# A spectral mix with a gated feed-forward block on one core: fewer first-layer passes for the value banks, and a fixed order of instructions

## The chip, the core and the metric

The kernel runs on one core of a Trainium2 chip. The metric is the device time of one execution in microseconds. TensorE multiplies matrices and accumulates in PSUM, which has eight banks here; VectorE, ScalarE and GpSimd work on elements (GpSimd on SBUF only); SyncE (SP) issues most of the DMA transfers. Each engine works through its own queue in order. An instruction that waits for another engine or for a transfer holds all that stands behind it in its queue.

## The reference

For each of 8 batches, x has 3008 rows of 256 columns:

```python
X = fft(fft(x, axis=1), axis=2);  y = X.real             # (8, 3008, 256)
g, v = y @ w_gate, y @ w_val                             # 256 -> 1536
out = (0.5*g*(1 + erf(g/sqrt(2))) * v) @ w_out           # 1536 -> 256
```

For real x the result has a symmetry: the spectrum at a row k and at the mirrored row 3008 - k share their parts. If E is the part of a gate or a value that is even in the columns and O the odd part, then row k has E + O, and the mirrored row has E - O, apart from one column of the odd half, the Nyquist column N (it lies in partition 0), which keeps its sign. So half of the rows, 1505 of them, suffice to compute both.

## The kernel before, in words

**Transform.** The rows of x are folded with their columns' mirror images (`fold_x`), on GpSimd in the main loop. The transform along the rows is done in two steps on TensorE: `a_step` (12 of them for a batch; lines 308 to 323) multiplies slices of the folded x (`xf`) with a table `G`, and the result goes by way of PSUM bank `ps_d` into `S1`. `z_write` writes `S1` to DRAM in eight transfers, four after the sixth step and four after the twelfth, and `z_read` reads it back, turned, into `Ap` in two transfers (the first holds the groups 0 to 15, the second 16 to 31). `b_steps` (lines 346 to 395) multiplies `Ap` with small tables and copies the result into `Y`, which has an even half and an odd half of 1505 columns.

**Feed-forward block.** The transform along the columns is multiplied into the weights at the start (`gen_w`): `WE` for the even half, `WOP` for the odd half, and `WOM`, which is -2 times `WOP` in all partitions but partition 0, where it is zero. The columns of `Y` are taken in three chunks of 512, 512 and 481. A *unit* is one batch, one chunk and one of 12 slices of the 1536 hidden columns; there are 8 x 3 x 12 = 288 units, 36 to a batch. `p1` computes the gate and the value for the plus rows, each as one pass with `WE` and one with `WOP` (lines 415 and 417), then GELU on ScalarE and the product on VectorE (lines 420 and 421) into `h`. `p2`, one unit later, adds one pass with `WOM` to each of the same two banks (line 431), which turns E + O into E - O, and again GELU and product (lines 435 and 436). So a unit has six first-layer passes on TensorE and two operations each on ScalarE and VectorE.

**Second layer.** When a chunk's 12 units are done, 96 matmuls of 256 columns (line 462) multiply `h` with the output weights; eight of them are put behind each of the next 12 units. After each 24, the result is copied by ScalarE and stored in four or five transfers.

**The next batch beside it.** While batch b is in the feed-forward block, units 0 to 11 each issue an `a_step` of batch b + 1, units 12 and 13 its `z_read`, and units 18 to 33 its `b_steps`, which are put between the unit's passes (`fill`). x of batch b + 2 is loaded and folded at units 0, 12 and 24, in pieces of eight slices.

**Order.** The order in which the program is written is not the order of the queues: a planner sorts the instructions of each engine by priority and by the time at which it expects them to be ready. So before the change a transform step whose data are late is planned behind other units' passes. Buffers: two PSUM banks for gates, three for values, two for the second layer, one for `ps_d`; two `h`, four `gl` (the GELU results), three `xin`.

Of the kernel before, what the change touches and what calls it, by code (L numbers as in the profile page):

```python
# [28 lines left out]
def kernel(  # L29
# [49 lines left out]
    Wo_sb = const_pool.tile([128, NFC, C], BF16)  # L79
    xf_bufs = [const_pool.tile([128, HJ, 2, 128], BF16, name=f"xf{i}") for i in range(2)]  # L80
# [31 lines left out]
    def gl_tile():  # L112
        return work.tile([128, 512], BF16, tag="gl", bufs=4, name="gl")
# [19 lines left out]

    xins = {}
# [17 lines left out]
    def fold_x(b, i, eng):  # L152
        j0, nj = PIECES[i]
        xt = xins[(b, i)]
        xf = xf_bufs[b % 2]
        parts = [(0, 128, 0, nj)]
        if j0 + nj == HJ:
            parts = [(0, 128, 0, nj - 1), (0, N1, nj - 1, 1)]
        for (p0, pn, s0, sn) in parts:
            o0 = (j0 + s0) * C  # L160
            lo = _sub(xt, [[C, sn], [1, 127]], s0 * C + 1, p0, pn)
            hi = _sub(xt, [[C, sn], [-1, 127]], s0 * C + 255, p0, pn)
            ea = _sub(xf, [[C, sn], [1, 127]], o0 + 1, p0, pn)
            od = _sub(xf, [[C, sn], [1, 127]], o0 + 129, p0, pn)
            eng.tensor_tensor(ea, lo, hi, op=ALU.add)  # L165
            eng.tensor_tensor(od, lo, hi, op=ALU.subtract)  # L166
            eng.tensor_copy(
                _sub(xf, [[C, sn], [128, 2]], o0, p0, pn),
                _sub(xt, [[C, sn], [128, 2]], s0 * C, p0, pn),
            )  # L170
# [35 lines left out]
    def scratch(n, name):  # L206
        return work.tile([128, n], FP32, tag=name, bufs=1, name=name)
# [75 lines left out]
    def gen_w():  # L283
        nc.vector.tensor_scalar(col_m, col_p, 1.0, -2.0, op0=ALU.is_ge, op1=ALU.mult)
        for i in range(2):
            wb = work.tile([128, NCH, F], BF16, tag="gw", bufs=2, name="wb")
            for t in range(NCH):
                wst["last"] = nc.gpsimd.tensor_copy(wb[:, t, :], wst[i][:, t, :])
            for f0 in range(0, F, 512):
                for eo in range(2):  # L290
                    ps = (ps_g, ps_v)[eo]()
                    for t in range(NCH):
                        nc.tensor.matmul(
                            ps, CW[:, t, eo, :], wb[:, t, f0 : f0 + 512],
                            start=(t == 0), stop=(t == NCH - 1))
                    if eo == 0:
                        nc.scalar.activation(WE[:, i, f0 : f0 + 512], ps, AF.Copy)
                    else:
                        nc.scalar.activation(WOP[:, i, f0 : f0 + 512], ps, AF.Copy)
                        nc.vector.tensor_scalar(  # L300
                            WOM[:, i, f0 : f0 + 512], WOP[:, i, f0 : f0 + 512], col_m, None,
                            op0=ALU.mult)

# [4 lines left out]
    def a_step(b, k):  # L308
# [6 lines left out]
        for i in range(2):  # L315
            jj = 2 * k + i
            st[b]["mm"] = nc.tensor.matmul(  # L317
                ps[:, i * C : (i + 1) * C], G[:, jj, :], _sub(xf, [[1, C]], jj * C),
                start=True, stop=True)
        dst = _sub(S1, [[1, 2 * C]], 2 * k * C)  # L320
        if k % 2:
            return nc.scalar.activation(dst, ps, AF.Copy)  # L322
# [23 lines left out]
    def b_steps(b, eo, q):  # L346
# [3 lines left out]
        def mm(gi, m1):  # L350
            def run():
# [9 lines left out]
                if g == 0:  # L361
                    t = T0P if even else T0Q
                    nc.tensor.matmul(ps[r, 0:N2], w, t[:, 0:N2], start=True, stop=True)
                    nc.tensor.matmul(ps[r, 8 * N2 : 8 * N2 + 1], w, t[:, N2 : N2 + 1],
                                     start=True, stop=True)
                else:
                    s = (36 * g) % N2
                    t = TP if even else TQ
                    nc.tensor.matmul(ps[r, o : o + N2], w, t[:, s : s + N2], start=True, stop=True)  # L369
            return run  # L370

        def evac():
# [5 lines left out]
            nc.vector.tensor_copy(  # L378
# [4 lines left out]
            nc.vector.tensor_copy(  # L383
                _sub(Y, [[32, n2], [1, 8 - f]], eo * YW + 32 * MID + g0 + f - 1),
                _sub(ps, [[1, n2], [N2, 8 - f]], MID + f * N2))
            if q == 0:
                nc.vector.tensor_copy(
                    _sub(Y, [[32, n2]], eo * YW + 32 * MID + 31), ps[:, MID:N2])
                nc.vector.tensor_copy(
# [15 lines left out]
    def p1(u, fill):  # L405
        b, ci, fc = units[u]
        c0, n = CH[ci]
        if fc == 0:
            hs[(b, ci)] = h_tile()
        h, Y = hs[(b, ci)], Ys[b]  # L410
        pg, pv = ps_g(), ps_v()
        banks[u] = (pg, pv)
        fs = slice(fc * 128, (fc + 1) * 128)
        for i, ps in enumerate((pg, pv)):
            nc.tensor.matmul(ps[:, :n], WE[:, i, fs], Y[:, 0, c0 : c0 + n], start=True, stop=False)  # L415
            fill()
            nc.tensor.matmul(ps[:, :n], WOP[:, i, fs], Y[:, 1, c0 : c0 + n], start=False, stop=True)  # L417
            fill()
        gl = gl_tile()
        nc.scalar.activation(gl[:, :n], pg[:, :n], AF.Gelu)  # L420
        nc.vector.tensor_tensor(h[:, fc, :n], gl[:, :n], pv[:, :n], op=ALU.mult)  # L421

    def p2(u, fill):
        b, ci, fc = units[u]
        c0, n = CH[ci]
        n -= n % 32
        h, Y = hs[(b, ci)], Ys[b]
        pg, pv = banks.pop(u)
        fs = slice(fc * 128, (fc + 1) * 128)
        for i, ps in enumerate((pg, pv)):  # L430
            nc.tensor.matmul(ps[:, :n], WOM[:, i, fs], Y[:, 1, c0 : c0 + n],  # L431
                             start=False, stop=True, skip_group_check=True)
            fill()
        gl = gl_tile()
        nc.scalar.activation(gl[:, :n], pg[:, :n], AF.Gelu)  # L435
        nc.vector.tensor_tensor(  # L436
            _sub(h, [[-1, n]], fc * 1024 + 512 + n - 1), gl[:, :n], pv[:, :n], op=ALU.mult)
# [6 lines left out]
    def l2_steps(b, ci):  # L444
# [5 lines left out]
        for sign in range(2):  # L450
            for pair in range(2):
                box = {}
                for s in range(2):
                    sub = 2 * pair + s
                    M = min(128, (n if sign == 0 else 32 * nm) - sub * 128)
                    for fc in range(NFC):
                        def run(sign=sign, pair=pair, s=s, sub=sub, M=M, fc=fc, box=box):
                            if "ps" not in box:
# [3 lines left out]
                            nc.tensor.matmul(  # L462
                                ps[:M, s * C : (s + 1) * C],
                                h[:, fc, sign * 512 + sub * 128 : sign * 512 + sub * 128 + M],
                                Wo_sb[:, fc, :], start=(fc == 0), stop=(fc == NFC - 1))
# [4 lines left out]
        def finish(sign, pair, M, ps):  # L470
            t = osb_tile()
            if M == 128:
                nc.scalar.activation(_sub(t, [[1, 2 * C]], 0), ps, AF.Copy)  # L473
            else:
                nc.scalar.activation(t[:, 0, :], ps[:, :C], AF.Copy)
                nc.scalar.activation(t[:M, 1, :], ps[:M, C:], AF.Copy)
# [46 lines left out]
    for q in range(4):  # L523
        for eo in range(2):
# [3 lines left out]
            evac()  # L528

# [3 lines left out]
    for u in range(NU + 1):  # L533
# [3 lines left out]
        if u < NU:  # L537
            if i % 12 == 0 and i < 36 and b + 2 < B:
                load_x(b + 2, i // 12)
                fold_x(b + 2, i // 12, nc.gpsimd)  # L540
            if b + 1 < B:
                if i < 12:
                    a_step(b + 1, i)
                    if i % 6 == 5:
                        z_write(b + 1, 2 * (i - 5), 12)
                elif i in (12, 13):
                    z_read(b + 1, 16 * (i - 12), 16)
                elif 18 <= i < 34:
                    k = i - 18
# [21 lines left out]

        if u < NU:
            p1(u, fill)
        if u > 0:
            p2(u - 1, fill)
# [4 lines left out]
        if u > 0 and u % 12 == 0:  # L580
            pb, pi = divmod(u // 12 - 1, 3)
            l2q += l2_steps(pb, pi)
        for _ in range(8 if u < NU else len(l2q)):
            if l2q:
                l2q.pop(0)()
# [30 lines left out]
```

## Time and profile before

| | |
|---|---|
| median of 3 runs | 739.55 us (735.27 to 741.46) |
| span of the profiled execution | 732.0 us (no other time is given for it) |
| TensorE busy | 695.4 us, 95% |
| VectorE, ScalarE, GpSimd busy | 473.2, 424.1, 113.1 us |
| chain of work that ended last | TensorE 92%, DMA 3%, VectorE 2% |
| passes of the first layer | 6 x 288, busy 108 us a line and bank |
| second layer, line 462 | 2304 matmuls, 298.6 us |

PE is TensorE, PEld its weight loads, DVE VectorE, ACT ScalarE, POOL GpSimd, SP SyncE. A row of a group gives line, engine, operation, output <- inputs, shapes and count, then the total busy time in us, the mean of one in ns, and the idle time in front of it with what ended it. Matmuls are pipelined: the duration of one (0.38 us) is longer than the distance to the next, so the distance of the starts gives the throughput. A row of the table by stage gives the stretch, its length, the busy time and count of each engine, then the TensorE clock granted (1.00 is full), the busy share of the DMA engines and GB/s. A row of the timeline gives start, duration, engine, line and operation. For SP the duration is that of issuing, not of the transfer.

### The profile page before, as it was taken

How to read it: one execution, taken by the hardware profiler on the slowest of the kernel's cores; microseconds unless marked ns; L12 is line 12 of the kernel's file. 1: busy time of each engine (PE TensorE's matmuls, PEld its weight loads, DVE VectorE, ACT ScalarE, POOL GpSimd, SP SyncE). 2: the span in 40 equal slices, each digit the busy share in tenths (PEclk: the TensorE clock that was granted, in tenths of full speed). 3: DMA queues.
4: the chain of work that ended last, by engine and by line, in shares of the span. 5: the costliest groups of instructions: out<-in, count | busy, mean ns of one | idle time of the engine just before them, and what ended most of it. 6: DMA issues, size and time to landing. Idle time of an engine off the chain costs nothing.

```text
span 732.0 us, 13929 instructions
## 1 busy us (share of the span) xinstructions
PE 695.4 (95%) x5040; PEld 439.7 (60%) x5040; DVE 473.2 (65%) x854; ACT 424.1 (58%) x761; POOL 113.1 (15%) x105
## 2 busy tenths in 40 slices
PE   1389999999999999999999999999999999999997
PEld 0145566666666666666666666666566666666666
DVE  7848676666667566666766666666666667665651
ACT  2347655666556655665556655566556665556662
POOL 1328220202205004400252003400000000000000
PEclk9989999999999999999999999999999999999999
DMA  8995841554444624544455535236111441111112
GB/s 180 275 240 131 216 98 30 143 136 123 98 114 117 169 64 121 123 116 126 100 141 137 142 88 130 56 85 167 35 39 35 123 121 43 30 44 41 43 45 69
DMA packets 63620, 79.29 MB, mean 108 GB/s; under 512 B 8256, under 2 KB 58432, under 8 KB 59456
## 3 DMA queue, kind: packets, MB, share of 16 engines
q1 hardware_dynamic: 61456, 74.48, 40.9%
q10 hardware_dynamic: 544, 3.15, 1.2%
q0 software_dynamic: 1552, 0.79, 0.9%
q8 instruction: 39, 0.64, 0.4%
q14 instruction: 29, 0.24, 0.1%
HBM read 41.94 MB, written 37.22 MB: 108 GB/s over the span
## 4 chain that ended last, share of the span: by engine, by line
PE 92%; DMA 3%; DVE 2%; SPq 1%; issue 0%; ACT 0%; ACTq 0%; DVEq 0%
PE ps_o L462 34%; PE ps_g L417 9%; PE ps_v L415 9%; PE ps_v L417 9%; PE ps_g L431 9%; PE ps_g L415 9%; PE ps_v L431 8%; PE ps_d L369 4%; PE ps_d L317 3%; DMA Ap<-z 2%; DMA xin<-in_x_dram 1%; SPq L334 1%; DMA z<-S 1%; DVE xf L166 0%; DVE xf L165 0%
## 5 line engine op out<-in xcount | busy, mean ns | idle before, releaser
L421 DVE TENSOR_TENSOR h<-gl,ps_v 128x512 bf16<-128x512 bf16 (+1 forms) x288 | 195.2, 678 | 214.4 <-ACT gl L420 102.5
L462 PE MATMUL ps_o<-Wo_sb,h 128*128 128x256 bf16 (+2 forms) x2304 | 298.6, 272 | 0.0
L462 PEld LDWEIGHTS <-h 128*128 128x128 bf16 (+2 forms) x2304 | 227.1, 100 | 81.8 <-issue 0.2
L420 ACT ACTIVATE gl<-ps_g 128x512 bf16<-128x512 f32 (+1 forms) x288 | 169.6, 589 | 169.3 <-PE ps_g L417 153.7
L436 DVE TENSOR_TENSOR h<-gl,ps_v 128x512 bf16<-128x512 bf16 (+1 forms) x288 | 194.1, 674 | 6.7 <-ACT gl L435 1.5
L435 ACT ACTIVATE gl<-ps_g 128x512 bf16<-128x512 f32 (+1 forms) x288 | 169.6, 589 | 35.6 <-PE ps_g L431 28.6
L415 PE MATMUL ps_g<-Y,WE 128*128 128x512 bf16 (+1 forms) x288 | 108.4, 377 | 0.7 <-ACT gl L435 0.3
L417 PE MATMUL ps_g<-Y,WOP 128*128 128x512 bf16 (+1 forms) x288 | 108.6, 377 | 0.0
L415 PE MATMUL ps_v<-Y,WE 128*128 128x512 bf16 (+1 forms) x288 | 108.4, 376 | 0.0
L417 PE MATMUL ps_v<-Y,WOP 128*128 128x512 bf16 (+1 forms) x288 | 108.3, 376 | 0.0
L431 PE MATMUL ps_g<-Y,WOM 128*128 128x512 bf16 (+1 forms) x288 | 107.8, 375 | 0.0
L431 PE MATMUL ps_v<-Y,WOM 128*128 128x512 bf16 (+1 forms) x288 | 107.5, 373 | 0.0
L165 POOL TENSOR_TENSOR xf<-xin 128x1016 bf16<-128x1016 f32 (+2 forms) x28 | 50.4, 1801 | 329.1 <-DMA xin<-in_x_dram 161.0
L431 PEld LDWEIGHTS <-WOM 128*128 128x128 bf16 x576 | 51.0, 97 | 51.4
L417 PEld LDWEIGHTS <-WOP 128*128 128x128 bf16 x576 | 56.1, 97 | 33.4 <-issue 3.6
L415 PEld LDWEIGHTS <-WE 128*128 128x128 bf16 x576 | 56.2, 98 | 30.9 <-issue 0.7
L473 ACT ACTIVATE osb<-ps_o 128x512 f32<-128x512 f32 x80 | 47.8, 597 | 42.6 <-PE ps_o L462 39.6
L369 PEld LDWEIGHTS <-Ap 96*128 96x128 bf16 (+1 forms) x744 | 39.8, 92 | 43.6 <-issue 24.4
L166 POOL TENSOR_TENSOR xf<-xin 128x1016 bf16<-128x1016 f32 (+2 forms) x28 | 50.4, 1800 | 0.0
L369 PE MATMUL ps_d<-TP,Ap 96*128 96x47 bf16 (+1 forms) x465 | 39.3, 185 | 1.8 <-DMA Ap<-z 1.7
L322 ACT ACTIVATE S<-ps_d 128x512 bf16<-128x512 f32 x42 | 25.0, 596 | 18.9 <-PE ps_d L317 18.9
L317 PEld LDWEIGHTS <-G 128*128 128x128 bf16 x192 | 19.5, 103 | 26.4 <-ACT G L233 19.0
(88 smaller groups left out, 251.1 us busy)
## 6 DMA issues: line engine op xcount, KB each, us to landing
out_dram<-osb SPq DMA_DIRECT2D x360, 64.0 KB, 1.7
xin<-in_x_dram SPq DMA_DIRECT2D x40, 512.0 KB, 6.6
z<-S SPq DMA_DIRECT2D x64, 192.0 KB, 3.1
Ap<-z SPq DMA_DIRECT2D x16, 768.0 KB, 7.9
xin<-in_x_dram SPq DMA_DIRECT2D x8, 448.0 KB, 6.4
wst<-in_moe_w_gate_dram ACTq DMA_DIRECT2D x1, 1536.0 KB
wst<-in_moe_w_val_dram ACTq DMA_DIRECT2D x1, 1536.0 KB
Wo_sb<-in_moe_w_out_dram POOLq DMA_DIRECT2D x1, 768.0 KB, 15.5
```

The lines of the kernel that those rows point to most:

```text
L165: eng.tensor_tensor(ea, lo, hi, op=ALU.add)
L166: eng.tensor_tensor(od, lo, hi, op=ALU.subtract)
L369: nc.tensor.matmul(ps[r, o : o + N2], w, t[:, s : s + N2], start=True, stop=True)
L415: nc.tensor.matmul(ps[:, :n], WE[:, i, fs], Y[:, 0, c0 : c0 + n], start=True, stop=False)
L417: nc.tensor.matmul(ps[:, :n], WOP[:, i, fs], Y[:, 1, c0 : c0 + n], start=False, stop=True)
L420: nc.scalar.activation(gl[:, :n], pg[:, :n], AF.Gelu)
L421: nc.vector.tensor_tensor(h[:, fc, :n], gl[:, :n], pv[:, :n], op=ALU.mult)
L431: nc.tensor.matmul(ps[:, :n], WOM[:, i, fs], Y[:, 1, c0 : c0 + n], start=False, stop=True, skip_group_check=True)
L435: nc.scalar.activation(gl[:, :n], pg[:, :n], AF.Gelu)
L436: nc.vector.tensor_tensor(_sub(h, [[-1, n]], fc * 1024 + 512 + n - 1), gl[:, :n], pv[:, :n], op=ALU.mult)
L462: nc.tensor.matmul(ps[:M, s * C : (s + 1) * C], h[:, fc, sign * 512 + sub * 128 : sign * 512 + sub * 128 + M], Wo_sb[:, fc, :], start=(fc ...
L473: nc.scalar.activation(_sub(t, [[1, 2 * C]], 0), ps, AF.Copy)
```

## The change

1. Two kinds of units. Kind 0 are every fourth unit (slices 0, 4 and 8) and all units of the first chunk of batch 0; they keep six passes. In kind 1 the value bank gets two passes: one with `WE`, and later one with `WOP`. In between, VectorE forms `ev` = E + N out of the bank, in fp32 (`NQ` is the row N in all partitions, `WN` its weight). After the second pass VectorE makes the plus product as before and then `dv` = 2 ev - (E + O), which is the minus value, in fp32. GpSimd multiplies `dv` with the GELU of the minus gate, one unit later.
2. `WN` is formed at the start by 24 matmuls of one column. `NQ` is filled once a batch by `spread_n`: one transfer writes the row to DRAM, one reads it into all 128 partitions. For batches after the first it is issued behind unit 31.
3. Every TensorE, VectorE, ScalarE and GpSimd instruction of the main loop is pinned: `pin` queues it behind all that was issued earlier in the program on its engine. The transfers are not pinned.
4. Order within a unit u: first value pass (or two) of u, the minus gate pass of u - 1, the two gate passes of u, the last value pass of u - 1, then the `a_step`, then eight second-layer matmuls. `b_steps` are put between them at units 16 to 31 instead of 18 to 33. The `a_step` stands at the end of its unit, no longer at the start. `z_write` and `z_read` stay at their units.
5. Folding goes in single slices, at units 4 to 11 of each twelve, behind the GpSimd product. In batches after the first, all copies into `S1` and `Y` go to ScalarE.
6. Buffers: eight `gl`, three `ev`, three `dv`; the scratch tiles of the start share `ev`, and the weights in transit share `Y`.

The core of the diff:

```diff
+    def pin(ins):
+        return tc.keep_in_program_order(ins) if held[0] else ins
...
+        ps = ps_o()
+        for fc in range(NFC):
+            for t in range(NCH):
+                nc.tensor.matmul(
+                    ps[:, fc : fc + 1], wb[:, t, fc * 128 : (fc + 1) * 128], CW[:, t, 1, 0:1],
+                    start=(t == 0), stop=(t == NCH - 1))
+        nc.vector.tensor_copy(WNb[:, :], ps[:, :NFC])
+        nc.vector.tensor_copy(WN[:, :], WNb[:, :])
+
+    def spread_n(b):
+        Y = Ys[b]
+        row = dram.tile([1, YW], BF16, tag="nrow", bufs=2, name="nrow")
+        nc.sync.dma_start(out=row[:, :NCOL], in_=_sub(Y, [[1, NCOL]], YW, 0, 1))
+        nc.sync.dma_start(
+            out=NQ[b % 2][:, :NCOL],
+            in_=ap_replace(row[:, :], ap=[[0, 128], [1, NCOL]], offset=row[:, :].offset))
...
-        if k % 2:
-            return nc.scalar.activation(dst, ps, AF.Copy)
+        if k % 2 or b > 0:
+            return pin(nc.scalar.activation(dst, ps, AF.Copy))
...
-    def p1(u, fill):
...
-    def p2(u, fill):
...
+    def kind(u):
+        b, ci, fc = units[u]
+        return 0 if (b == 0 and ci == 0) or fc % 4 == 0 else 1
...
+    def val_even(u):
+        r = banks[u]
+        r["pv"] = ps_v()
+        layer1(r, r["pv"], WE, 1, 0, r["n"], True)
+        if r["kd"]:
+            nm, fc = r["nm"], r["fc"]
+            r["ev"] = ev_tile()
+            pin(nc.vector.scalar_tensor_tensor(
+                r["ev"][:, :nm], r["nq"][:, r["c0"] : r["c0"] + nm], WN[:, fc : fc + 1],
+                r["pv"][:, :nm], op0=ALU.mult, op1=ALU.add))
+        else:
+            layer1(r, r["pv"], WOP, 1, 1, r["n"], False)
+
+    def gate_minus(u):
+        r = banks[u]
+        layer1(r, r["pg"], WOM, 0, 1, r["nm"], False)
+        r["glm"] = gl_tile()
+        pin(nc.scalar.activation(r["glm"][:, : r["nm"]], r["pg"][:, : r["nm"]], AF.Gelu))
+
+    def gate_plus(u, fill):
...
+        layer1(r, r["pg"], WE, 0, 0, n, True)
+        fill()
+        layer1(r, r["pg"], WOP, 0, 1, n, False)
+        fill()
+        r["glp"] = gl_tile()
+        pin(nc.scalar.activation(r["glp"][:, :n], r["pg"][:, :n], AF.Gelu))
...
+    def val_odd(u):
...
+        if r["kd"] == 0:
+            layer1(r, pv, WOM, 1, 1, nm, False)
+            pin(nc.vector.tensor_tensor(hm, r["glm"][:, :nm], pv[:, :nm], op=ALU.mult))
+        else:
+            layer1(r, pv, WOP, 1, 1, r["n"], False)
+            plus(r)
+            dv = dv_tile()
+            pin(nc.vector.scalar_tensor_tensor(
+                dv[:, :nm], r["ev"][:, :nm], 2.0, pv[:, :nm], op0=ALU.mult, op1=ALU.subtract))
+            r["dv"] = dv
+
+    def minus(u):
...
+            pin(nc.gpsimd.tensor_tensor(hm, r["glm"][:, :nm], r["dv"][:, :nm], op=ALU.mult))
...
-    for u in range(NU + 1):
+    held[0] = True
+    for u in range(NU + 2):
...
+                if 16 <= i < 32:
+                    k = i - 16
...
         if u < NU:
-            p1(u, fill)
-        if u > 0:
-            p2(u - 1, fill)
+            val_even(u)
+            fill()
+        if 0 < u <= NU:
+            gate_minus(u - 1)
+            fill()
+        if u < NU:
+            gate_plus(u, fill)
+            if banks[u]["kd"] == 0:
+                plus(banks[u])
+        if 0 < u <= NU:
+            val_odd(u - 1)
         while fills:
             fill()
         if after:
             after()
+        if u > 1:
+            minus(u - 2)
+        if u < NU:
+            if i % 12 >= 4 and b + 2 < B:
+                fold_x(b + 2, i // 12, nc.gpsimd, i % 12 - 4, 1)
+            if b + 1 < B:
+                if i < 12:
+                    a_step(b + 1, i)
+                    if i % 6 == 5:
+                        z_write(b + 1, 2 * (i - 5), 12)
+                elif i in (12, 13):
+                    z_read(b + 1, 16 * (i - 12), 16)
+                if i == 31:
+                    spread_n(b + 1)
```

## The prediction

> **What bounds the kernel now.** First the page's busy times, then the table by stage, to see whether a mean hides stages.
>
> ```profile
> PE 695.4 (95%) x5040; PEld 439.7 (60%) x5040; DVE 473.2 (65%) x854; ACT 424.1 (58%) x761; POOL 113.1 (15%) x105
> ```
>
> ```profile
> 20.00:40.00 20.00, 8.25 (x27) 3.20 (x28) 14.27 (x26) 9.23 (x20) 6.95 (x5) 1.00 1.02 263
> 40.00:60.00 20.00, 16.44 (x154) 9.05 (x153) 12.55 (x34) 9.34 (x17) 8.79 (x5) 0.83 1.02 229
> 200.00:300.00 100.00, 100.00 (x738) 63.61 (x735) 65.50 (x116) 59.77 (x107) 19.81 (x15) 1.00 0.46 116
> ```
>
> From about 52 us TensorE is never idle, at full clock; VectorE and ScalarE have a third free. A TensorE pass taken out of the loop is time saved, and a new TensorE wait is time lost. The timeline of the last batch gives the price of a pass:
>
> ```profile
> 660.65 0.38 PE L415 MATMUL ps_g<-Y,WE 128*128 128x512 bf16 x1
> 660.87 0.38 PE L417 MATMUL ps_g<-Y,WOP 128*128 128x512 bf16 x1
> 661.09 0.38 PE L415 MATMUL ps_v<-Y,WE 128*128 128x512 bf16 x1
> 661.95 1.04 PE L462 MATMUL ps_o<-Wo_sb,h 128*128 128x256 bf16 x8
> 662.82 0.38 PE L415 MATMUL ps_g<-Y,WE 128*128 128x512 bf16 x1
> ```
>
> The 0.38 us are latency; starts count. Six passes take 660.65 to 661.95, 0.217 us each; eight second-layer matmuls 0.87 us, 0.109 each; a unit 2.17 us. In the short chunk six passes take 1.22 us (709.86 to 711.08), 0.203 each.
>
> **What goes.** Units of kind 1 have five passes instead of six. Nine in twelve units are of kind 1, except in the first chunk of batch 0: 63 + 72 long and 72 short ones. 135 x 0.217 + 72 x 0.203 = 43.9 us. All of it is on the path.
>
> **VectorE.** A kind-1 unit has three operations there (sum with the Nyquist row, plus product, difference) for two. The trace has no scalar_tensor_tensor from PSUM; near rows:
>
> ```profile
> L421 DVE TENSOR_TENSOR h<-gl,ps_v 128x512 bf16<-128x512 bf16 x192 | 131.9, 687 | 139.8 <-ACT gl L420 78.1 <-PE ps_g L431 51.6 <-PE ps_v L417 9.5
> L221 DVE SCALAR_TENSOR_TENSOR sc<-sb,sa 128x512 f32<-128x512 f32 x3 | 2.0, 680 | 0.0
> ```
>
> Queued operations of this size start every 0.60 us (copies from PSUM at 24.36, 24.96, 25.56), so one costs 0.60 to 0.69 us; I take 0.60. Four units need 3 x 3 + 2 = 11 operations, 6.6 us (7.6 at the upper end); TensorE takes 2.17 + 3 x 1.95 = 8.0 us for them where it does nothing else. The tightest place is the value bank of the unit before one of kind 0: its difference waits behind a product that needs the new gate, ends 3.8 us after that unit began, and the bank is wanted at 4.1. It holds at 0.60 and just at 0.69: nothing, hidden by TensorE's own 8.0 us; above 0.73 us an operation (8.0 / 11) that cover is gone, and 72 such groups of four wait 0.11 us for each 0.01 us more. In the first chunk of batch 0 (no second layer, 1.52 us a unit) the same sum comes out some 0.13 us late a unit: 1.4 us. VectorE is relieved of the later copies of S1 and Y; ScalarE, which takes them, has queued 512-element copies every 0.48 us, at most 3.3 operations in 2.2 us: nothing.
>
> **GpSimd.** It gets 207 products and the folds in single slices, in strict order. Nearest rows:
>
> ```profile
> L165 POOL TENSOR_TENSOR xf<-xin 128x1016 bf16<-128x1016 f32 x14 | 32.8, 2342 | 197.8 <-DMA xin<-in_x_dram 67.0 <-PE ps_o L462 44.9 <-PE ps_g L417 33.4
> L165 POOL TENSOR_TENSOR xf<-xin 64x127 bf16<-64x127 f32 x7 | 3.1, 448 | 81.0 <-DMA xin<-in_x_dram 43.8 <-PE ps_d L369 19.6 <-PE ps_g L417 17.7
> ```
>
> From 0.45 us for 127 to 2.34 us for 1016 is 2.13 ns an element, so a product is about 1.27 us (bounds 0.6, VectorE's, and 2.34); a folded slice is 0.95 us from start to start. Twelve units: 9 x 1.27 + 8 x 0.95 = 19 us against at least 24 on TensorE. Nothing, unless a product takes over (24 - 7.6) / 9 = 1.8 us. The loads for the folds stand far ahead in SP's queue. The Trainium skill (GPSIMD Engine Reference, Engine selection) speaks against this move: elementwise work with two inputs belongs on VectorE, being about half as fast on GpSimd. The rows agree on the ratio (2.34 us here, 1.22 for the same fold on VectorE at the start), but by this sum it is not the wait that ends last.
>
> **What the fixed order costs.** Here I expect the gain to go. The steps of the next batch now stand at set places in TensorE's queue, and a step that waits for data holds all passes behind it.
>
> (a) *First transform step.* The first step for batch 1 stands behind the first unit's four passes. They start at 49.24 and, at half clock as before, end at 50.95; the step needs x of batch 1 folded:
>
> ```profile
> 55.80 0.24 POOL L167 CAST xf<-xin 128x16 bf16<-128x16 f32 x1
> ```
>
> It starts at 56.05 instead: 5.1 us. Before, TensorE did other units meanwhile.
>
> (b) *The way through DRAM.* The second transform begins at unit 16 instead of 18, in shorter units, and the last first-transform step stands late in unit 11. Before:
>
> ```profile
> 579.71 0.38 PE L317 MATMUL ps_d<-xf,G 128*128 128x256 bf16 x2
> 580.75 2.08 SPq L334 DMA_DIRECT2D z<-S  x4
> 582.97 2.38 SPq L442 DMA_DIRECT2D out_dram<-osb  x4
> 585.61 0.79 SPq L344 DMA_DIRECT2D Ap<-z  x2
> ...
> 597.71 0.19 PE L363 MATMUL ps_d<-T0P,Ap 96*128 96x47 bf16 x1
> ```
>
> From the last step to the issue of the reload 5.9 us; the first half lands 5.9 us after its issue (the two landings here are 5.9 and 7.9): the data are there 11.8 us after the step, and 18.0 us were given. In the new order 40 second-layer matmuls, 23 passes and the step itself lie between: 40 x 0.109 + 23 x 0.217 + 0.22 = 9.55 us. All four z writes, the four stores and the reload keep their order on SP; ScalarE's copy comes some 0.15 us later, behind a gate. So TensorE waits 2.4 us, with new x loads beside the reload somewhat more: I take 3.0, six times, 18 us (bounds 2.4 and, with the longest lag in this trace, 7.3 us from 323.20 to 330.52, 3.9 each). In batch 0, x loads stand in front of the reload, whose first half took 9.2 us, and unit 11 has no second layer: 6.0 + 9.2 - 8.7 = 6.5 us.
>
> (c) *The clock.* The stages around the start show what idleness does; columns are TensorE busy, clock, DMA:
>
> ```profile
> 41.00:42.00 1.00, 0.43 (x2) 1.00 0.96 233
> 42.00:43.00 1.00, 0.28 (x11) 1.00 0.96 215
> 44.00:45.00 1.00, 0.74 (x20) 1.00 1.06 231
> 45.00:46.00 1.00, 0.00 (x0) 0.57 1.06 222
> 51.00:52.00 1.00, 1.00 (x4) 0.52 1.13 262
> 52.00:53.00 1.00, 1.00 (x6) 1.00 0.96 197
> ```
>
> With two pauses of 1.3 and 1.7 us the clock was halved at 45.15, and full again only at 51.97. Half clock for some 3.4 us (half of that stretch) costs 1.7 us. I count 2 us behind each of the two long waits and 1.15 behind each of the six short ones (three in four halve the clock, 1.5 us each): 10.9 us (bounds 0 and 8 x 3.4 = 27). The Trainium skill (TensorE: Matmul & The Clock Gate, section The HAM clock gate) lets the clock fall only after a whole idle window of about 3.4 us. By that rule the short waits cost no clock and this sum would be 4 us; the row at 45 us shows a fall with no such pause.
>
> New small things: 24 one-column matmuls lie in TensorE's pause before 42.7; the Nyquist row's two transfers have 10 us from unit 32 to the second unit of the next batch, against 8 for a larger reload: nothing for both.
>
> **Sum**, against the span 732.0: -43.9 + 5.1 + 18 + 6.5 + 1.4 + 10.9 = -2.0, or 730.0. The runs shown have a median of 739.55, 7.5 us above the span of the profiled execution, of which no other time is given; the same step from the median is 737.5. One per cent is about what can be told from no change here.
>
> **Rivals.**
> *The short waits leave the clock alone* (they are 2.4 us and fall across two periods of the throttle). For it: the fall at 45.15 had 3 us of pauses and thin matmuls around it. Against it: neither pause was long. -6.9 and 6 x -0.6: 727, faster by 1.7%.
> *The reload is no wait*, because the new loop is slower before unit 16 or the transfer faster. Then -43.9 + 5.1 + 1.4 + 2 = -35.4: 704. Against it: 5.9 + 5.9 us are the shortest in the trace.
> *The reload is later* (slower). If in batches 1 to 6 it lands as late as in batch 0, 9.2 us, each wait is 3.3 us longer, and half of that again in clock: some 20 to 30 us, 757 to 767. It decides from 1.6 us more per wait (746.9). For it: x loads, the row's transfers and stores share 16 DMA engines; against it: in the scheduled order these x loads follow the reload.
> *GpSimd binds* (slower): a product above 1.8 us. At 2.34, twelve units need 28.7 us; the batch 85 instead of 80, which mostly replaces the reload's wait: 738 to 755.
>
> **Chances.** Forecast 0.40 (own range 729 to 747), clock kept 0.27, no wait 0.06, later reload 0.19, GpSimd or VectorE binding 0.08. Faster by over 1% (below 732.2): 0.06 + 0.24 and a tail of the forecast, 0.35; slower (above 746.9) 0.17 + 0.06 and a tail, 0.25. For eight in ten I leave out the case without a wait and the far end of the late reload: 722 to 757.
>
> **What the profile will show.** TensorE waiting for the first folded x, about 5 us; for Ap seven times, 2.4 to 6.5 us each; granted clock below 1 in about eight places; units of kind 1 that start 1.95 us apart in the last batch; VectorE operations 0.6 us apart when queued; GpSimd products of 1.2 to 1.3 us. No waits for Ap would make the prediction too slow by up to 33 us; products above 1.8 us, VectorE operations above 0.73, or plain units above 2.0 us would make it too fast.

## The result, and the profile after

The changed kernel has a median of 743.01 us (740.55 to 746.34, 20 runs), the kernel before, run beside it, 740.44 us (733.20 to 744.22, 20 runs). The ratio is 1.0056, with an interval from 1.0029 to 1.0083: the change costs half a per cent, where it was forecast to gain a little (737.5, range 722 to 757).

The page of the changed kernel, busy times (span 744.5 us):

```profile
PE 672.8 (90%) x4857; PEld 426.7 (57%) x4857; DVE 524.9 (71%) x881; ACT 454.7 (61%) x943; POOL 397.7 (53%) x672
```

TensorE has 22.6 us less to do than before (672.8 against 695.4), although 207 passes are gone, worth 43.9 us; its share of the span fell from 95% to 90%. So it does less, some of it at half clock, and stands more. The waits of TensorE say where (total in us, times, longest):

```profile
PE ps_d L396 <- DMA Ap<-z: 33.2, 8, 7.8
...
PE ps_d L350 <- POOL xf L184: 6.2, 1, 6.2
```

Before, the loop had no such waits; the only one for `Ap` was that of batch 0's own start, which is 1.9 of the 33.2 here. In the timeline the idle time in front of an instruction stands in brackets:

```profile
57.41 0.58 PE L350 MATMUL ps_d<-xf,G 128*128 128x256 bf16 x2 [6.16 <-POOL xf L184]
94.23 0.22 PE L396 MATMUL ps_d<-T0P,Ap 96*128 96x47 bf16 x1 [7.81 <-DMA Ap<-z]
180.11 0.20 PE L396 MATMUL ps_d<-T0P,Ap 96*128 96x47 bf16 x1 [3.18 <-DMA Ap<-z]
...
610.61 0.20 PE L396 MATMUL ps_d<-T0P,Ap 96*128 96x47 bf16 x1 [3.72 <-DMA Ap<-z]
```

Line 350 is the first `a_step` for batch 1 and line 396 the first instruction of `b_steps`. The six waits from 180 to 611 us are 3.18, 4.31, 3.69, 3.86, 4.72 and 3.72 us: 23.5 together, one per batch.

Behind such a wait the clock falls. The table by stage around the one at 180 us (the clock is the third number from the end):

```profile
179.00:180.00 1.00, 0.00 (x0) 0.00 (x0) 0.00 (x0) 0.00 (x0) 0.39 (x2) 1.00 1.04 246
180.00:181.00 1.00, 0.89 (x9) 0.53 (x10) 0.00 (x0) 0.39 (x1) 0.00 (x0) 1.00 0.93 221
181.00:182.00 1.00, 1.00 (x7) 0.64 (x5) 0.00 (x0) 0.78 (x2) 0.00 (x0) 0.64 0.88 228
182.00:183.00 1.00, 1.00 (x5) 0.59 (x4) 0.94 (x2) 0.03 (x1) 0.00 (x0) 0.50 1.29 427
183.00:184.00 1.00, 1.00 (x7) 0.45 (x6) 1.00 (x3) 0.18 (x1) 0.00 (x0) 0.50 1.02 213
184.00:185.00 1.00, 1.00 (x5) 0.46 (x4) 0.60 (x1) 0.66 (x2) 0.91 (x1) 0.65 0.27 57
```

TensorE is busy from 180.1 on, at half clock from about 181.3 to 184.7. Busy time times (1 - clock), summed over such rows, is the time lost: 1.7 us here, 18.0 us in the whole execution (2.7 before, all of it at the start). The other engines came out about as forecast. Groups of the changed kernel by shape (x count, then busy us and mean ns of one, then the idle time before):

```profile
L519 POOL TENSOR_TENSOR h<-gl,dv 128x512 bf16<-128x512 bf16 x135 | 157.0, 1163 | 207.8 <-DVE dv L510 141.2 <-ACT gl L492 46.0 <-ACT osb L555 15.9
L471 DVE SCALAR_TENSOR_TENSOR ev<-nq,WN,ps_v 128x512 f32<-128x512 bf16 x135 | 100.2, 742 | 2.3 <-PE ps_v L460 2.3
L510 DVE SCALAR_TENSOR_TENSOR dv<-ev,ps_v 128x512 f32<-128x512 f32 x135 | 91.7, 679 | 0.0
```

And two starts of plain units of kind 1 in the last batch, 1.95 us apart, as reckoned:

```profile
701.45 0.38 PE L460 MATMUL ps_v<-Y,WE 128*128 128x512 bf16 x1
...
703.40 0.38 PE L460 MATMUL ps_v<-Y,WE 128*128 128x512 bf16 x1
```

### The profile page after: what moved, and what is told of

Same layout as the page of the kernel before. It is cut to its first block, busy times and chain, and to the rows that moved or that the text cites. A ratio compares the mean times of both kernels' runs of the same rounds, so it can differ in the third digit from the quotient of the medians.

```text
span 744.5 us, 14403 instructions
## 1 busy us (share of the span) xinstructions
PE 672.8 (90%) x4857; PEld 426.7 (57%) x4857; DVE 524.9 (71%) x881; ACT 454.7 (61%) x943; POOL 397.7 (53%) x672
## 4 chain that ended last, share of the span: by engine, by line
PE 84%; DMA 10%; DVE 2%; SPq 2%; POOL 1%; issue 1%; ACT 0%; ACTq 0%; DVEq 0%; POOLq 0%
PE ps_o L544 33%; PE ps_g L460 25%; PE ps_v L460 19%; DMA Ap<-z 6%; PE ps_d L402 4%; DMA xin<-in_x_dram 3%; PE ps_d L350 3%; SPq L524 1%; DMA z<-S 0%; DVE xf L183 0%; PE ps_d L396 0%; DVE xf L182 0%; ACT gl L481 0%; DVE sc L238 0%; SPq L367 0%
## 5 line engine op out<-in xcount | busy, mean ns | idle before, releaser
L519 POOL TENSOR_TENSOR h<-gl,dv 128x512 bf16<-128x512 bf16 (+1 forms) x207 | 236.4, 1142 | 287.1 <-DVE dv L510 198.4
L496 DVE TENSOR_TENSOR h<-gl,ps_v 128x512 bf16<-128x512 bf16 (+1 forms) x288 | 188.8, 675 | 185.0 <-ACT gl L492 143.7
L544 PE MATMUL ps_o<-Wo_sb,h 128*128 128x256 bf16 (+2 forms) x2304 | 302.2, 276 | 0.0
L544 PEld LDWEIGHTS <-h 128*128 128x128 bf16 (+2 forms) x2304 | 230.3, 101 | 64.0 <-issue 3.7
L471 DVE SCALAR_TENSOR_TENSOR ev<-nq,WN,ps_v 128x512 f32<-128x512 bf16 (+1 forms) x207 | 151.0, 730 | 2.3 <-PE ps_v L460 2.3
L510 DVE SCALAR_TENSOR_TENSOR dv<-ev,ps_v 128x512 f32<-128x512 f32 (+1 forms) x207 | 138.3, 668 | 0.0
L182 POOL TENSOR_TENSOR xf<-xin 128x127 bf16<-128x127 f32 (+3 forms) x148 | 72.6, 490 | 22.6 <-DMA xin<-in_x_dram 22.6
L402 PEld LDWEIGHTS <-Ap 96*128 96x128 bf16 (+1 forms) x744 | 50.2, 94 | 58.5 <-issue 32.5
L183 POOL TENSOR_TENSOR xf<-xin 128x127 bf16<-128x127 f32 (+3 forms) x148 | 72.7, 491 | 0.0
L505 DVE TENSOR_TENSOR h<-gl,ps_v 128x512 bf16<-128x512 bf16 (+1 forms) x81 | 54.3, 670 | 3.2 <-PE ps_v L460 3.1
L355 ACT ACTIVATE S<-ps_d 128x512 bf16<-128x512 f32 x84 | 50.6, 603 | 6.5 <-DMA xin<-in_x_dram 6.2
L402 PE MATMUL ps_d<-TP,Ap 96*128 96x47 bf16 (+1 forms) x465 | 49.5, 188 | 2.4 <-DMA Ap<-z 2.2
```

The source lines that it names most:

```text
L182: pin(eng.tensor_tensor(ea, lo, hi, op=ALU.add))
L183: pin(eng.tensor_tensor(od, lo, hi, op=ALU.subtract))
L402: pin(nc.tensor.matmul(ps[r, o : o + N2], w, t[:, s : s + N2], start=True, stop=True))
L471: pin(nc.vector.scalar_tensor_tensor(r["ev"][:, :nm], r["nq"][:, r["c0"] : r["c0"] + nm], WN[:, fc : fc + 1], r["pv"][:, :nm], op0=ALU.mul ...
L496: pin(nc.vector.tensor_tensor(r["h"][:, r["fc"], :n], r["glp"][:, :n], r["pv"][:, :n], op=ALU.mult))
L505: pin(nc.vector.tensor_tensor(hm, r["glm"][:, :nm], pv[:, :nm], op=ALU.mult))
```

## The experiments

The theory after the result: the passes are worth their 43.9 us, and the set places of the transform steps in TensorE's queue give it back, as waits for the reload of `Ap`, one wait for the first fold, and half clock behind them. Each part was taken away by itself.

### The reload given two units more

```diff
-                if 16 <= i < 32:
-                    k = i - 16
+                if 18 <= i < 34:
+                    k = i - 18
...
-                if i == 31:
+                if i == 33:
                     spread_n(b + 1)
```

> The changed kernel with the second transform's steps at units 18 to 33 (as before the change) instead of 16 to 31, and the Nyquist row spread behind unit 33. Theory (the reload wait and the halved clock behind it eat the gain): two more units of 1.95 us stand in front of the reload's reader, so the six waits of 3.2 to 4.7 us (23.5 us in all) go to 0 to 0.8 us each, the wait of batch 0 from 7.8 to some 4 us, and most of the 15 us of clock come back: 743 - 23 - 4 - 11 = about 705 us. Rival (the five-pass unit itself is slow, on VectorE or GpSimd): the waits move elsewhere and the time stays within 10 us, 733 to 743 us.

Measured: 720.23 us, 0.9734 of the kernel before (0.967 to 0.980). That is 23 us less than the changed kernel, not the 38 expected. Its waits of TensorE and VectorE (the profile is of the longest of its four runs, 724.97 us):

```profile
DVE ev L471 <- DMA nq<-nrow: 18.1, 5, 4.0
...
PE ps_v L460 <- DVE ev L471: 13.2, 5, 3.1
...
PE ps_d L396 <- DMA Ap<-z: 7.5, 4, 3.8
```

The reload is hardly a wait any more after batch 0 (0.16 and 0.49 us where there is one; 3.8 in batch 0). Another has taken its place: `ev` needs the Nyquist row of the new batch, which leaves only behind unit 33 now, and at the next batch's first units of kind 1 VectorE stands for it and TensorE, which wants the bank, behind VectorE. So there were two deadlines on the same chain, reload to steps to row, and moving the steps by two units broke the second to keep the first.

### The odd halves first

```diff
-                    q, r = divmod(k, 4)
-                    if r == 0:
-                        st[b + 1]["cur"] = b_steps(b + 1, 0, q)
...
+                    q, r = divmod(k % 8, 2)
+                    if r == 0:
+                        st[b + 1]["cur"] = b_steps(b + 1, 1 if k < 8 else 0, q)
...
-                if i == 33:
+                if i == 26:
                     spread_n(b + 1)
```

> The second step of the transform at units 18 to 33 (as in the run of 720.2 us), and in it the odd halves first: units 18 to 25 do the four odd quarters, units 26 to 33 the four even ones, and the Nyquist row is sent out behind unit 26 instead of 33. No work is added or taken away. Theory: what is left of waiting in the loop of the 720.2 us kernel is the row that comes too late for the next batch's first kind-1 units (TensorE stood 13.2 us in 5 waits behind VectorE's ev, which waited for nq), with three dips of the clock of 1.7 us each behind it; both go: 720.2 - 13.2 - 5.1 = 702 us, 699 to 706. Rival: those waits are VectorE's or the DMA queue's own, and the row comes late wherever it is sent from, or the second half of Ap, now read 4 units earlier, is late in its place: 715 to 725.

Measured: 704.12 us (703.15 to 705.34), 0.954 (0.947 to 0.961): as expected. The wait for `ev` is gone (its five waits and the three dips of the clock behind them), and the halves of `Ap` come nearly in time: in the loop TensorE waits for them twice, 0.9 us each, and 3.0 us in batch 0. This says that the row's late departure was the cause, not VectorE and not the transfer.

### The start, too

```diff
-                if i < 12:
-                    a_step(b + 1, i)
+                if b == 0:
+                    if 5 <= i < 11:
+                        for k in (2 * (i - 5), 2 * (i - 5) + 1):
+                            a_step(1, k, (ps_d, ps_o)[k % 2])
+                            if k % 6 == 5:
+                                z_write(1, 2 * (k - 5), 12)
+                    elif i in (11, 12):
+                        z_read(1, 16 * (i - 11), 16)
+                elif i < 12:
+                    a_step(b + 1, i)
```

> The kernel with the odd halves first, and in batch 0 the twelve first steps for batch 1 go two to a unit at units 5 to 10 (one in the bank of its own, one in a bank of the second layer, which is idle then) instead of one to a unit at 0 to 11; the write of S1 and the reload come one unit earlier. Theory: the wait for the folded x at the first unit (6.75 us) and the reload wait of batch 0 (3.8 us) are waits for transfers and folds that are under way anyway, so they go without another taking their place, and the dips of the clock behind them too (1.8 and 2.6 us): about 15 us less than the kernel with the odd halves first, 687 us, 684 to 692. Rival: the first chunk is bound by the folds on GpSimd and, with two evictions more in a unit, by ScalarE, so the waits only move: 697 to 706.

Measured: 694.43 us (694.17 to 695.71), 0.9416 (0.936 to 0.947). The page and the waits of this kernel (span 692.2 us):

```profile
PE 655.3 (95%) x4857; PEld 421.9 (61%) x4857; DVE 524.7 (76%) x881; ACT 454.2 (66%) x943; POOL 397.0 (57%) x672
```

```profile
PE ps_d L396 <- DMA Ap<-z: 5.7, 1, 5.7
...
PE ps_d L402 <- DMA Ap<-z: 1.9, 1, 1.9
PE ps_v L460 <- DVE h L505: 0.7, 3, 0.2
```

TensorE is back at 95%, and no wait above 0.2 us is left in the loop: the 5.7 and 1.9 us lie at 43 and 47 us, where batch 0's own `Ap` is read. It saved 9.7 us where 15 were expected, since the waits that it removes were smaller in the kernel it was built on (5.2 and 3.0 us, where I had put in the 6.75 and 3.8 of the one before); with 3.4 us of clock (7.7 lost there, 4.3 here) that is 11.6, and the spans of the two profiles differ by 11.4. This version keeps the passes of the change and its pinned order, and is 42 us faster than the kernel before by the runs beside it (median 736.81). Its span of 692.2 stands against 732.0 - 43.9 = 688.1: once nothing waits in the loop, nearly all of the 43.9 us are there.

### The clock alone

```diff
+    def warm(u, n):
+        ps = ps_d()
+        for _ in range(n):
+            pin(nc.tensor.matmul(
+                ps[:, :512], WE[:, 0, 0:128], banks[u]["Y"][:, 0, 0:512], start=True, stop=True))
...
+            if b + 1 < B and i == 16:
+                warm(u, 14 if b else 30)
```

> The changed kernel with extra matmuls of no use (14 of 512 columns, 30 in batch 0) put in front of the waiting step at unit 16, which TensorE does while it would wait. Theory (the clock falls behind the waits, and this costs time): the waits end when they ended, but the clock stays full: seven times 1.5 to 2.5 us less, about 731 us. Rival (the low granted clock behind the waits costs nothing, because TensorE has slack there): 743 us, within 3.

The matmuls added are work whose results nobody reads. Measured: 731.11 us (730.38 to 734.30), 0.988 (0.982 to 0.994). TensorE at the wait of batch 1, and the table by stage behind it:

```profile
174.18 3.19 PE L480 MATMUL ps_d<-Y,WE 128*128 128x512 bf16 x14
177.43 0.18 PE L396 MATMUL ps_d<-T0P,Ap 96*128 96x47 bf16 x1
```

```profile
178.00:179.00 1.00, 1.00 (x9) 0.71 (x8) 0.00 (x0) 0.78 (x2) 0.00 (x0) 1.00 0.85 243
179.00:180.00 1.00, 1.00 (x12) 0.65 (x10) 0.64 (x2) 0.36 (x2) 0.00 (x0) 1.00 1.33 454
180.00:181.00 1.00, 1.00 (x8) 0.67 (x7) 1.00 (x3) 1.00 (x3) 0.00 (x0) 1.00 0.95 197
```

The data come hardly sooner: from the last `a_step`, at 164.64, to line 396 are 12.8 us, as in the changed kernel (167.22 to 180.11), and over the six batches 12.8 to 14.0, against 12.9 to 14.4 there. But the clock stays up.

The loss by the clock is 4.9 us, all at the start, against 18.0 us in the changed kernel and 14.2 in a second profile of it (further below): 13.1 and 9.3 us less. The medians differ by 11.9 us. So the half clock behind the waits is real time, on top of the waits.

### The fixed order without the saved passes

```diff
     def kind(u):
-        b, ci, fc = units[u]
-        return 0 if (b == 0 and ci == 0) or fc % 4 == 0 else 1
+        return 0
```

> The changed kernel with all units of kind 0: same fixed order, six passes everywhere. Theory (a pass is worth 0.217 us on the path, and the loss is that of the order): 207 passes come back, 43.9 us, less 0.65 us of every reload wait, since the three units in front of it grow: 743 + 43.9 - 4.5 = about 782 us. Rival (a good part of the 43.9 us never was a gain, because VectorE or GpSimd set the pace of kind 1): 750 to 770 us.

Measured: 774.80 us, 1.0471 (1.0403 to 1.0539). Its wait for the reload:

```profile
PE ps_d L396 <- DMA Ap<-z: 27.0, 8, 6.8
```

So the order, with its earlier second transform and the other parts of the change, costs 34 us by itself, and the passes bring back 31.8 of them (774.80 less 743.01). They are worth 43.9. The rest shows in the profiles. The span here is 772.1 us, against 744.5 and 738.1 in the two profiles of the changed kernel, 27.6 and 34.0 us more. With six passes more in the way, the data are waited for 6.2 and 5.2 us less (27.0 against 33.2 and 32.2), and the clock loses 6.1 and 2.3 us less (11.9 against 18.0 and 14.2). That makes 39.9 and 41.5 us, so 2 to 4 of the 43.9 are not accounted for. Where the end of a wait is set by a transfer, work taken out in front of it comes back as waiting. The time lies between the 782 expected and the rival's 770: I had counted 4.5 us less waiting, and nothing for the clock.

### The saved passes without the fixed order

```diff
     l2q = []
-    held[0] = True
     for u in range(NU + 2):
```

> The changed kernel without the pins: the planner sorts the main loop. In the order that results, TensorE has 35 us of other work between the last first-transform step and the reader of the reload. Theory: no wait for the reload, none for the first fold, no halved clock after 52 us: 743 - 37 - 15 = about 691, with some us back for waits on banks, 690 to 705 us. Rival (the five-pass units need the fixed order: in the planner's order value banks and the GpSimd products come late): 730 us or more.

Measured: 739.60 us (735.34 to 745.43, 10 runs), 1.0006 (0.996 to 1.006): the rival's time was right, and half of its reason. In the loop TensorE waits neither for `Ap` nor for the fold, nor for a value bank. Instead:

```profile
PE ps_g L460 <- ACT gl L481: 24.9, 24, 4.2
...
PE ps_g L460 <- ACT gl L492: 6.2, 6, 3.2
```

and on ScalarE, the wait behind that:

```profile
ACT gl L481 <- POOL h L519: 36.6, 24, 4.4
```

The gate bank waits for GELU, GELU for a free `gl` buffer, and the buffer for GpSimd's product, in front of which GpSimd does folds. GpSimd at 228 to 232 us:

```profile
228.18 1.17 POOL L519 TENSOR_TENSOR h<-gl,dv 128x512 bf16<-128x512 bf16 x1 [0.63 <-DVE dv L510]
229.30 0.46 POOL L182 TENSOR_TENSOR xf<-xin 128x127 bf16<-128x127 f32 x1
...
232.02 0.20 POOL L184 CAST xf<-xin 128x2 bf16<-128x2 f32 x1
232.16 1.18 POOL L519 TENSOR_TENSOR h<-gl,dv 128x512 bf16<-128x512 bf16 x1
```

Three slices in a row stand between two products, where the pinned order has one. The waits of 31.1 us, with 9.8 us more of half clock than in the kernel before (12.5 lost against 2.7), use up nearly all of the 43.9. So in this order the folds seem to take what the reload takes in the other; that they alone are the cause was not tried by itself. The versions above show that the pins need not cost anything, if the steps stand where their data are there.

### The product on VectorE

```diff
-            pin(nc.gpsimd.tensor_tensor(hm, r["glm"][:, :nm], r["dv"][:, :nm], op=ALU.mult))
+            pin(nc.vector.tensor_tensor(hm, r["glm"][:, :nm], r["dv"][:, :nm], op=ALU.mult))
```

> The changed kernel with one edit: the minus product of the 135 kind-1 units on VectorE instead of GpSimd. Theory (the place on GpSimd is needed): VectorE's work in four plain units goes from 3 x 1.85 + 1.2 = 6.75 us to 6.75 + 3 x 0.60 = 8.55 us, over the 7.74 us that TensorE needs, 0.2 us a unit in the some 80 plain units and nothing in the units with steps of the transform between: 743 + 16 = 759 us, 750 to 770, VectorE's busy time some 525 + 85 = 610 us. Rival (the page's rule that work which either engine can do goes to VectorE): the product takes less than 0.45 us there, TensorE stays the bound, and the time is within 743 +- 4 us or below.

Measured: 755.73 us (753.87 to 756.59), 12.7 us over the changed kernel. (There are 207 such products; the 135 are those of full width. So VectorE's busy time is 649 us, not 610.) VectorE in the last batch:

```profile
705.19 0.68 DVE L510 SCALAR_TENSOR_TENSOR dv<-ev,ps_v 128x512 f32<-128x512 f32 x1
705.79 0.68 DVE L519 TENSOR_TENSOR h<-gl,dv 128x512 bf16<-128x512 bf16 x1
706.39 0.74 DVE L471 SCALAR_TENSOR_TENSOR ev<-nq,WN,ps_v 128x512 f32<-128x512 bf16 x1
```

A product starts 0.60 us before the next operation, against 1.16 us on GpSimd. The ratio of the Trainium skill (GPSIMD Engine Reference, Engine selection: about half as fast on GpSimd) holds here. But VectorE is then without a gap in this stretch, and four units take 8.57 us (701.67 to 710.24) where the changed kernel takes 8.02. For the changed kernel the slower engine is the right place.

### The two levels of the kernel before

The runs of the kernel before lie in two groups, spans of some 731 to 735 and some 737 to 743 us; the profile that the prediction was summed on is of the lower one. A second profile of the same kernel:

> The kernel before once more, unchanged, for a second profile of it. Its 13 timed runs beside the first experiments lie on two levels: three spans of 731.0 to 733.5 us at a mean granted clock of 0.993 to 0.995, and ten of 737.4 to 743.0 us, nine of these at 0.987 to 0.991. The profile that the prediction was summed on (span 732.0, clock 0.995) is one of the low ones. Theory: the two levels are the clock itself; in a run of the upper level the records show two or three low-clock stretches more than the single one at 45 to 52 us, and the low clock times the span accounts for most of the difference (0.007 x 740 = 5 us of 7). Rival: the clock stretches are the same and a transfer of the start lands 6 us later. If this run falls on the lower level again, the question stays open.

Measured: span 742.1 us, on the upper level. The clock is the smaller part of it. Its waits have a long one that the first profile has not, and its list of transfers shows why (the last number is the time to landing; it was 15.5 in the first profile):

```profile
PE ps_o L462 <- DMA Wo_sb<-in_moe_w_out_dram: 7.2, 1, 7.2
```

```profile
Wo_sb<-in_moe_w_out_dram POOLq DMA_DIRECT2D x1, 768.0 KB, 29.1
```

The output weights were issued at 33.5 us instead of 31.2, and the loads of x followed at 35.7. They landed after the second layer's first matmul was due; TensorE stood 7.2 us, and lost 6.4 us by the clock instead of 2.7. 7.2 + 3.7 = 10.9, against 10.1 between the spans (732.0 and 742.1). Then the load was moved:

```diff
                 wst["last"] = nc.gpsimd.tensor_copy(wb[:, t, :], wst[i][:, t, :])
+            if i == 0:
+                with tc.issue_after(wst["last"].ins):
+                    load_wo()
```

> The kernel before with one edit: the load of the output weights stands on GpSimd's queue behind the first weight's two casts instead of behind all four, some 6 to 8 us earlier; every other queue has the same order. Theory: the two levels of the kernel before come from this load. In the profile with span 732.0 it was issued at 31.2 and landed after 15.5 us, ahead of the second layer's first matmul at 54.4; in the one with span 742.1 it was issued at 33.5, shared the DMA engines with the loads of x (issued from 35.7), landed after 29.1 us, and TensorE stood 7.2 us for it with a half clock from 60 to 67 us behind. Issued at 24 to 25 it lands by 53 in any case, and all runs are at 730 to 736 us, none above 737. Rival: the late landing belongs to a slower start of another cause (both casts were late too), and an earlier load only takes bandwidth from the weights in front of it: the runs still lie on two levels, median 738 to 742.

Measured: 737.22 us (736.00 to 738.22, 10 runs; 0.997, 0.993 to 1.0005). The upper level is gone: 2.2 us from the lowest run to the highest, where the kernel before beside it had 9.3 (734.27 to 743.55). But all ten lie above the lower level; in the profile the first read of `Ap` is waited for 4.8 us instead of 1.3, so there is some of the rival in it. The late load makes the upper level, as far as one profile of that level and these ten runs show; moving it costs some 2 us against the lower one (735.45 in the middle of its five runs here).

In the changed kernel it doesn't matter: the weights land after 29.1 us, at 61.3, and the second layer begins at 79.1. A second profile of it:

> The changed kernel once more, unchanged, for a second profile; the first, with a span of 744.5 us, was the longest of its 20 runs. The sum of its measured terms, 732.0 - 43.9 + 37.5 (waits) + 15.3 (clock), is 740.9, so 3.6 us are left over. Theory: they are not one place but the slower refilling behind each wait, and this run has them too: span less the sum of its own terms again 2 to 5 us. Rival: they are chance of the one execution: below 1 us here. The load of the output weights lands ahead of the second layer's first matmul (79 us) whether it takes 15 or 29 us, without a wait of TensorE for it.

Measured: span 738.1 us. The waits are 6.5 (fold), 7.2 (batch 0) and 23.0 (six batches), the clock loses 14.2 us, 11.6 more than before: 732.0 - 43.9 + 36.7 + 11.6 = 736.4, and 1.7 are left over. That is neither what the theory nor what the rival said, but the kernel without waits in the loop has about as much left over (732.0 - 43.9 + 1.7 of clock is 689.8; its span is 692.2, and its first unit starts 0.9 us later, at 50.15 instead of 49.24). So what is left over is not refilling behind waits; some 0.7 us of it are the small waits for VectorE in the first chunk, the rest stays open.

## Why the prediction was wrong

It said 737.5, with faster, same and slower about even, and named the place where the gain would go. The direction was wrong: the sum came out 2 us below its base, the span of 732.0. The median of the changed kernel, less the 1.8 us by which a run is longer than its span, is 741.2, 9 us above it. The terms, in us against the span 732.0, with the two profiles of the changed kernel, of which the first is the longest of its 20 runs and the second shorter than all of them:

| term | forecast | first profile | second |
|---|---|---|---|
| 207 passes | -43.9 | -43.9 | -43.9 |
| first folded x | 5.1 | 6.2 | 6.5 |
| reload, six batches | 18 | 23.5 | 23.0 |
| reload, batch 0 | 6.5 | 7.8 | 7.2 |
| clock | 10.9 | 15.3 | 11.6 |
| first chunk, rest | 1.4 | 3.6 | 1.7 |
| sum | -2.0 | 12.5 | 6.1 |

**Right:** the passes (shown by the units' distance, by the one without waits, and to within 4 us by the kernel with six passes); VectorE's 0.60 us an operation (`ev` 0.65); GpSimd's product (1.27 forecast, 1.16 measured) and that neither engine binds; each wait by its place, and no other; that short waits can halve the clock.

**Step (b) failed by its size,** and it is the largest miss: 23.5 and 23.0 us instead of 18. I took 5.9 us from the last `a_step` to the issue of the reload. The chain in the changed kernel, batch 1:

```profile
167.22 0.38 PE L350 MATMUL ps_d<-xf,G 128*128 128x256 bf16 x2
```

```profile
168.43 2.63 SPq L367 DMA_DIRECT2D z<-S  x4
171.16 2.82 SPq L524 DMA_DIRECT2D out_dram<-osb  x4
174.16 0.79 SPq L377 DMA_DIRECT2D Ap<-z  x2
```

That is 6.94 us, and 5.95 more until TensorE goes on at 180.11. The 9.55 us of work between were nearly right (180.11 - 3.18 - 167.22 = 9.71, the same in all six). The 5.9 of the landing were right for the first two of the six; the other four are 6.5 to 6.7, and the mean is 6.36, inside the margin of 0.6 that I had added. The six lags are 6.94, 8.09, 6.93, 6.92, 7.74 and 6.93: mean 7.26. In the trace of before the same six are 6.99, 6.25, 7.32, 6.38, 5.99 and 5.90: mean 6.47, and I had built on the last, the shortest of all. With the mean the wait would have been 3.0, with a margin 3.6; it was 3.9 (7.26 + 6.36 - 9.71), which the prediction held as its upper bound. The new order adds 0.8 us to the mean lag: the first `z_write` comes 0.17 us later behind the last step (1.21 instead of 1.04), and the eight transfers in front of the reload take 6.05 instead of 5.43 us on the mean. Why they take longer stays open.

**The waits of step (a) and of batch 0** came out 1.1 to 1.4 and 0.7 to 1.3 us longer. For step (a), x of batch 1 was folded that much later (57.1 and 56.9 us in the two profiles, 55.8 in the trace of before). That is in part a difference of single executions: the second profile of the kernel before has 56.6, the kernel with the odd halves first 55.9. In batch 0 the lag was 6.7 us instead of 6.0, and the landing 10.1 and 9.4 instead of 9.2.

**Step (c), the clock,** was right in kind. I had three in four short waits halve the clock at 1.5 us each; in the first profile all six did, at 1.8 on average, in the second four of six, 1.2 a wait. The rule of the Trainium skill that I set against it (TensorE: Matmul & The Clock Gate, section The HAM clock gate), a fall only after a whole idle window of about 3.4 us, would have given 4 us for waits of 3.0. Five of the six waits of the first profile were longer than that window, so they say little against the rule. The one of 3.18 us does, at 180 us, and shorter ones do in other runs: 2.27 us in the kernel with six passes (shown below). The measurement decides here. The rival that short waits leave the clock alone was stated for waits of 2.4 us, which the changed kernel has not; with the pauses of 2.27 to 2.43 us in other runs the clock fell in two cases of five.

**The base failed, too, in the other direction.** I carried the step of -2.0 over to the median, by adding the 7.5 us between it and the span. A run takes only 1.8 us more than its span (743.89 against 742.1). The other 5.7 were the level: the usual run of before, as far as its one profile shows, waits for the output weights, and the first profiled one did not, and the changed kernel, whose second layer starts 25 us later, can't wait for them. Summed rightly it would have been 732.0 - 2.0 + 1.8 = 732; the terms were 11 us short, and the base hid half of that. So it is by luck that 737.5 is no further from the 743.0 measured.

## What to carry to other kernels

A step whose data come by a transfer, pinned into an in-order queue, has a deadline: follow the chain from its last producer to it over every batch of the trace and take the mean or the long end, not the shortest. Work that is taken out between the producer and the reader shortens the cover; give the reader its place by the new length of the units, and then look for the next reader down the chain, which has a deadline as well. And before a sum is made against one profile, see whether the spans of the timed runs are in one group: if they are not, find the wait that makes the second group, since the change may remove it or not.

## What the runs showed of the hardware beyond that

The low-clock stretches come in multiples of some 3.4 us (3.4, 6.8, 10.2 and 17.1 in these profiles). Whether a pause brings one on is not set by its length alone: after the pause at 176.9 to 180.1 us of the first profile the clock was halved for 3.4 us; after nearly the same pause in the second, 175.8 to 178.8, it stayed full:

```profile
178.00:179.00 1.00, 0.20 (x4) 0.19 (x5) 0.00 (x0) 0.00 (x0) 0.50 (x2) 1.00 1.02 262
179.00:180.00 1.00, 1.00 (x9) 0.53 (x7) 0.00 (x0) 0.60 (x1) 0.00 (x0) 1.00 1.03 254
180.00:181.00 1.00, 1.00 (x12) 0.80 (x11) 0.25 (x1) 0.60 (x1) 0.00 (x0) 1.00 0.89 274
```

Nor does it take 3 us. In the kernel with six passes everywhere, one of 2.27 us, ended at 182.92, halved it from about 183:

```profile
182.92 0.22 PE L396 MATMUL ps_d<-T0P,Ap 96*128 96x47 bf16 x1 [2.27 <-DMA Ap<-z]
```

```profile
182.00:183.00 1.00, 0.08 (x2) 0.09 (x3) 0.00 (x0) 0.00 (x0) 0.00 (x0) 0.96 1.05 262
183.00:184.00 1.00, 1.00 (x8) 0.45 (x9) 0.00 (x0) 0.33 (x1) 0.00 (x0) 0.50 1.02 254
```

Counted over all twelve profiles, from 60 us on: every one of the 24 pauses of TensorE of 3.48 to 7.81 us brought half clock, during the pause or up to 1.2 us behind it. Of the 18 pauses of 2.27 to 3.19 us nine did and nine did not, and of the 14 of 0.66 to 1.31 us none did. What decides in the middle range stays open.
